# Sliding-window attention and a feed-forward layer on one core: the fourth chunk's scores as fp16 pairs, planned durations and two weight steps changed

## The chip, the core and the metric

The kernel runs on one core of a Trainium2 chip. The metric is device time in microseconds (us) of one execution; lower is better. Three runs of the kernel before gave 631.44, 631.64 and 631.9 us, median 631.64 us. About 0.2% (1.3 us) is what a measurement of this kernel can tell from no change.

## The reference

```python
# q, k, v: (4, 8, 768, 64) float32, n_sink = 4, window = 128
scores = q @ k.T / sqrt(64)
keep = (key < n_sink) | (0 <= query - key < window)
a = softmax(where(keep, scores, -1e9))
x = (a @ v) transposed to (3072, 512)
h = x @ w_in                      # (512, 2048)
g = where(h > 0, h, exp(min(h, 0)) - 1)
out = g @ w_out                   # (2048, 512)
```

The two weights come as 64-bit floats; q, k and v as 32-bit floats.

## The kernel before, in words

**Tiles and chunks.** The 3072 tokens are 24 tiles of 128, cut into nine chunks (`SIZES`, line 43): three of two tiles, then six of three. For each chunk, `attention(c)` (line 495) makes the rows of x, 4 pairs of heads one after the other, and `feed_forward(c, f0, f1, start)` (line 753) runs over 16 blocks of 128 hidden units: `stage1` (line 759) makes h in 12 products of x with a block of w_in, the ELU follows on ACT, DVE and POOL (lines 773 to 786), and `stage2` (line 788) adds the block's products with w_out into one PSUM bank per tile. Both layers work on fp16 pairs: a 32-bit value is kept as a high fp16 half and the fp16 rest, and three products stand for one. Chunks 0 and 1 are cut in two parts (`PARTS`, line 46), so that their first blocks can run while later weights are still being prepared. Attention of a chunk runs beside the feed-forward of the chunk before it.

**Scores.** `DUP` (line 50) says how a chunk's scores are made. In the first `DUP` chunks (line 513 and lines 598 to 601), keys and queries of two heads are loaded as 32-bit floats, one head in partitions 0 to 63, the other in 64 to 127, and used as they are: two fp32 products for a tile and a pair of heads, both listed under line 601. In the later chunks each head has a load of its own (line 523) with the head in both halves of the partitions; ACT writes the high halves (line 524), DVE the rests of the keys (line 525) and of the queries (line 526), and each head's scores are two fp16 products (lines 595 and 596). With `DUP` = 4 the fourth chunk (three tiles, 12 pairs of tile and head pair) is the last with fp32 scores. At the end of the program `check_kq` (line 842) loads the keys and queries of the later chunks again and takes their largest value (line 851).

**Softmax.** DVE adds the mask and takes the extremum (line 616), ACT the exponential with its sum (line 618), a small step scales the sum (line 622, on ACT or POOL) and DVE inverts it (line 623). In chunk 0 POOL builds a diagonal matrix of the inverses (line 630), PE turns the weights with it (line 636), and ACT or DVE evacuates (line 640). In the later chunks ACT and DVE write fp16 pairs (lines 668, 669), POOL the sink columns (lines 675 to 679), and a DMA transposes (line 687). PE multiplies with the values (lines 653 and 701 to 706), and ACT and DVE write x as a pair (lines 739, 740).

**Weights.** `weights(k)` (line 441) prepares 32 pieces of 128 x 512. A 512 KB load on SP's queue (line 314) is followed by four steps: ACT turns the top bits into a fp16 number (line 307, in `weight_f32`), DVE ors the other bits into it, which gives a 32-bit float (line 308), ACT writes the high half (line 456), and POOL the rest in two halves of 256 columns (line 457).

**The order.** Nothing of this order is written by hand. Each step is a task with an engine, an assumed duration and its dependencies (`add`, line 112); `or_=` names a second engine that may take it. `Plan.order` (line 138) works backward for due times and forward for start times, PE's tasks in fixed lines by position, the others by due time, in 8 rounds, and keeps the plan that ends first. What it found is then the fixed order of every engine and of SP's queue: an engine runs its instructions in this order, and one that waits holds all behind it. In a plan, POOL and those steps of DVE that are marked `slow` over 1 take turns (lines 249 to 267). Where the plan sees PE idle for over 0.8 us in its first 100 us, `with_idle_products` (line 896) fills 0.6 of the gap with products of a constant that nobody reads (line 882).

**The end.** One branch at the end (line 1142) skips a general path that takes over when inputs are out of range. `HINTS` (line 891) says how many tasks before the end of each engine's program an instruction is placed that tells the engine of that branch ("notice" below; `keep_order`, line 930). The profile lists it as BRANCH_PREFETCH_HINT on line 1168.

Of the kernel before, what the change touches and what calls it, by code (L numbers as in the profile page):

```python
# [10 lines left out]
F16 = mybir.dt.float16  # L11
# [9 lines left out]
P = 128  # L21
# [27 lines left out]
VISIT = 3  # L49
DUP = 4  # L50
AHEAD = 5
# [4 lines left out]
T_AT = 3.5  # L56
PE_T, PE_V = 0.25, 0.25
RINGS = dict(tp=2, tp_=2, kqs=2, kq=3, vs=2, vm=2, vt=6, sk=2, e=3, st=6, pq=3, pt=6, g=2, gh=3, x=7, wv=4, s=2, po=1, h=2, wu=2, sv=2, wps=1, raw=6)
# [225 lines left out]
def act_us(n, scaled=False):  # L284
    return 0.17 + 0.00088 * n + (0.08 if scaled else 0.0)
# [80 lines left out]
def fast_path(tc, ctx, first, kq, vx, wt, out, low, spread, numbers, flag):  # L366
# [74 lines left out]
    def weights(k):  # L441
        raw, v = raws[slot("raw")], wv[slot("wv")]

        top = wu[k % RINGS["wu"]]
        ld = add("SP", 0.4, lambda: load_weights(nc, raw, wt[k]), deps=[w_done.get(k - AHEAD, [None])[0]], lat=1.45)
        if wide:
            steps = weight_f32(nc, v, top, raw, 2.0)
            a = add("ACT", act_us(512), steps[0], deps=[ld])
            b = add("DVE", 0.13 + 0.00108 * 512, steps[1], deps=[a], slow=1.5)
            ring("wu", [a], [b])  # L450
            ring("raw", [ld], [a, b])
        else:
            a = b = add("ACT", act_us(512), lambda: nc.scalar.activation(v, raw[:, :512].bitcast(F32), AF.Copy, scale=W_SCALE), deps=[ld])
            ring("raw", [ld], [a])

        th = add("ACT", act_us(512), lambda: nc.scalar.activation(w[k][:, 0, :], v, AF.Copy), deps=[b])  # L456
        tls = [add("POOL", pool_us(256), lambda c=c: nc.gpsimd.tensor_tensor(w[k][:, 1, c], v[:, c], w[k][:, 0, c], ALU.subtract), deps=[th]) for c in (slice(0, 256), slice(256, 512))]  # L457
        tl = tls[-1]
        ring("wv", [b], tls)
        w_done[k] = th, *tls  # L460
# [34 lines left out]
    def attention(c):  # L495
# [74 lines left out]
        for p in range(NP):  # L570
# [5 lines left out]
            for g in ts:  # L576
# [47 lines left out]
                if c < PLAIN:  # L624
# [12 lines left out]

                    dgs = add("POOL", pool_us(2 * P), diagonal, deps=[rr])
                    tr = add("PE", PE_T * 2 * nb, turned, deps=[dgs], pos=at[k] + T_AT, line=3)
# [32 lines left out]
                if t >= 2:  # L672

                    def sinks(e3=e3, rs=rs, tmp=tmp, pq=pq):
                        nc.gpsimd.tensor_tensor(tmp, e3[:, :, 0:NS], rs.unsqueeze(2).to_broadcast([P, 2, NS]), ALU.mult)
                        hi = pq[:, 8, 0:96].rearrange("p (g r) -> p g r", g=3)[:, :, 0 : 2 * NS]
                        flat = tmp.rearrange("p e k -> p (e k)")
                        nc.gpsimd.tensor_copy(hi[:, 0:3:2, :], flat.unsqueeze(1).to_broadcast([P, 2, 2 * NS]))
                        nc.gpsimd.tensor_tensor(hi[:, 1, :], flat, hi[:, 0, :], ALU.subtract)

                    b = add("POOL", 0.65, sinks, deps=[rr], lock=False)
                    parts.append(b)
                    his.append(b)
# [54 lines left out]
            to_x = X_SCALE / P_SCALE if c < PLAIN else PO_SCALE  # L738
            fa = add("ACT", act_us(qc, True), lambda xh=xh, po=po, to_x=to_x: nc.scalar.activation(xh, po[:, :qc], AF.Copy, scale=to_x), deps=[vals[-1]])
            fb = add("DVE", dve_us(qc) + 0.1, lambda xh=xh, xl=xl, po=po, to_x=to_x: nc.vector.scalar_tensor_tensor(xl, po[:, :qc], to_x, xh, ALU.mult, ALU.subtract), deps=[fa])  # L740
            ring("po", [vals[0]], [fa, fb])
# [148 lines left out]

HINTS = dict(PE=8, ACT=120, DVE=120, SP=25)
E = mybir.EngineType
# [279 lines left out]
```

## Time and profile before

| what | value |
| --- | --- |
| time, median of 3 runs | 631.64 us |
| profiled execution, its own time | 632.12 us |
| its span in the trace | 630.3 us |
| PE busy, share of the span | 608.5 us, 97% |
| DVE, ACT, POOL busy | 451.4, 418.8, 291.2 us |
| chain that ended last: PE's share | 90% |
| products of the constant (line 882) | 29 |

A span is from the first to the last instruction of the trace; 1.8 us of the profiled execution lie around it. Engines: PE does matrix products, DVE, ACT and POOL work element by element, SP issues the DMAs. A PE that is busy can be waiting inside a product, so the distance from one product's start to the next is the better measure of what it costs.

### The profile page before, as it was taken

The page shows a single profiled execution, that of the slowest core. Times are in us where ns is not written, and L with a number is a line of the kernel's source. Part 1 is how long each engine was busy: PE and PEld are TensorE (multiplying, and loading weights), DVE is VectorE, ACT ScalarE, POOL GpSimd, SP SyncE. Part 2 cuts the span into 40 slices and gives each one's busy share as a digit, 9 for nine tenths or more (in the row PEclk, how much of TensorE's full clock was granted, in tenths as well). Part 3 has the DMA queues.
Part 4 walks back from the last instruction along what each step waited for, and adds up shares of the span by engine and source line. Part 5 has one row for each costly group of instructions (what it writes and reads, how often), then busy time and mean ns, then how long its engine had stood idle before and what let it go on. Part 6 is the DMA issues. An engine that isn't in the chain of part 4 may idle for free.

```text
span 630.3 us, 13327 instructions
## 1 busy us (share of the span) xinstructions
PE 608.5 (97%) x4504; PEld 357.1 (57%) x4504; DVE 451.4 (72%) x1187; ACT 418.8 (66%) x1192; POOL 291.2 (46%) x586
## 2 busy tenths in 40 slices
PE   6897999999999999999999999999999999999995
PEld 4564665666666555555555555555555555555552
DVE  7876677868678766688788889788778887542223
ACT  5888887978678866677667767676776676332221
POOL 4885699864345444344334444334334444222221
PEclk9998999999999999999999999999999999999998
DMA  8697967656546765486458865676556854511001
GB/s 288 212 254 189 305 233 208 161 165 176 120 120 137 194 104 103 88 220 174 103 168 189 208 158 148 145 193 144 154 118 134 220 130 100 124 56 30 0 2 54
DMA packets 120863, 95.06 MB, mean 151 GB/s; under 512 B 98132, under 2 KB 98132, under 8 KB 120788
## 3 DMA queue, kind: packets, MB, share of 16 engines
q1 hardware_dynamic: 120788, 94.14, 58.5%
q8 instruction: 37, 0.61, 0.4%
q14 instruction: 38, 0.31, 0.2%
HBM read 63.18 MB, written 7.34 MB: 112 GB/s over the span
## 4 chain that ended last, share of the span: by engine, by line
PE 90%; POOL 4%; DVE 2%; issue 2%; DMA 1%; ACT 0%; POOLq 0%; DVEq 0%; ACTq 0%
PE acc L793 39%; PE h L765 38%; PE po L701 5%; PE s L601 3%; PE s L595 2%; PE s L596 2%; POOL w L457 2%; DMA pt<-pq 1%; PE h L882 1%; DMA vs<-in_vx_dram 1%; POOL pq L630 1%; PE po L706 1%; DVE pt L334 0%; PE acc L636 0%; DVE wv L308 0%
## 5 line engine op out<-in xcount | busy, mean ns | idle before, releaser
L765 PE MATMUL h<-x,w 128*128 128x384 f16 (+1 forms) x1728 | 275.0, 309 | 1.5 <-DVE g L776 1.5
L765 PEld LDWEIGHTS <-w 128*128 128x128 f16 x1728 | 167.8, 98 | 94.9 <-issue 3.4
L786 POOL TENSOR_TENSOR gl<-g,gh 128x384 f16<-128x384 f32 (+1 forms) x144 | 126.0, 876 | 164.1 <-ACT gh L779 142.4
L793 PE MATMUL acc<-w,gh 128*128 128x512 f16 x768 | 192.8, 379 | 1.0 <-POOL w L457 1.0
L773 ACT ACTIVATE g<-h 128x384 f32<-128x384 f32 (+1 forms) x144 | 65.2, 453 | 102.2 <-PE h L765 93.0
L793 PEld LDWEIGHTS <-gh 128*128 128x128 f16 x768 | 72.4, 98 | 70.8 <-ACT g L773 1.4
L793 PE MATMUL acc<-w,gl 128*128 128x512 f16 x384 | 109.2, 379 | 0.0
L669 DVE SCALAR_TENSOR_TENSOR pq<-e,st,pq 128x256 f16<-128x256 f32 (+1 forms) x176 | 95.5, 569 | 15.0 <-ACT pq L668 14.7
L618 ACT ACTIVATE e<-e,st 128x264 f32<-128x264 f32 (+1 forms) x192 | 92.9, 485 | 14.9 <-DVE st L616 14.0
L779 ACT ACTIVATE gh<-g 128x384 f16<-128x384 f32 (+1 forms) x144 | 69.5, 482 | 45.2 <-DVE g L776 43.3
L616 DVE CUSTOM_DVE_ANT_0 e<-s,m 128x264 f32<-128x264 f32 (+1 forms) x192 | 71.8, 405 | 32.8 <-PE s L596 21.5
L776 DVE SCALAR_TENSOR_TENSOR g<-g,h 128x384 f32<-128x384 f32 (+1 forms) x144 | 72.9, 506 | 14.2 <-POOL g L775 12.4
L668 ACT ACTIVATE pq<-e,st 128x256 f16<-128x256 f32 (+1 forms) x176 | 77.5, 482 | 5.1 <-DVE st L623 4.3
L775 POOL TENSOR_SCALAR g<-g 128x384 f32<-128x384 f32 (+1 forms) x79 | 43.2, 547 | 79.1 <-ACT g L773 75.8
L775 DVE TENSOR_SCALAR g<-g 128x384 f32<-128x384 f32 (+1 forms) x65 | 27.1, 417 | 69.0 <-ACT g L773 68.9
L793 PEld LDWEIGHTS <-gl 128*128 128x128 f16 x384 | 37.5, 98 | 46.7 <-POOL gl L786 0.9
L457 POOL TENSOR_TENSOR w<-wv,w 128x256 f16<-128x256 f32 x64 | 48.9, 786 | 6.1 <-ACT w L456 5.5
L524 ACT ACTIVATE kq<-kqs 128x912 f16<-128x912 f32 (+1 forms) x40 | 35.8, 912 | 15.9 <-PE s L596 13.6
L622 POOL TENSOR_SCALAR st<-st 128x2 f32<-128x2 f32 x76 | 19.1, 251 | 49.4 <-ACT e L618 46.0
L701 PE MATMUL po<-pt,vh 128*64 128x128 f16 x656 | 36.1, 222 | 3.4 <-DVE x L740 1.9
L618 ACT ACTIVATION_READ_ACCUMULATOR e<-e,st 128x1 f32 x192 | 36.1, 188 | 0.0
L701 PEld LDWEIGHTS <-vh 128*64 128x64 f16 x656 | 26.6, 109 | 14.6 <-issue 14.0
(92 smaller groups left out, 619.4 us busy)
## 6 DMA issues: line engine op xcount, KB each, us to landing
raw<-in_wt_dram SPq DMA_DIRECT2D x32, 512.0 KB, 4.6
kqs<-in_kq_dram SPq DMA_DIRECT2D x24, 456.0 KB, 3.9
kqs<-in_kq_dram SPq DMA_DIRECT2D x20, 390.0 KB, 3.6
vs<-in_vx_dram SPq DMA_DIRECT2D x28, 256.0 KB, 3.8
out_dram<-wv SPq DMA_DIRECT2D x24, 256.0 KB, 3.0
vm<-in_kq_dram SPq DMA_DIRECT2D x24, 228.0 KB, 4.2
vm<-in_vx_dram SPq DMA_DIRECT2D x6, 768.0 KB, 5.3
vm<-in_kq_dram SPq DMA_DIRECT2D x16, 195.0 KB, 3.7
```

Of the source, the lines that this page charges most:

```text
L616: red = add("DVE", 0.24 + 0.001 * wd, lambda ee=ee, me=me, sp=sps[e], m=m, wd=wd, to_score=to_score: nc.vector.tensor_tensor_reduce(ee, sp ...
L618: ex = add("ACT", 0.47 + 0.00085 * wd, lambda ee=ee, me=me, rs=rs[:, e : e + 1]: nc.scalar.activation(ee, ee, AF.Exp, bias=me, scale=-1.0, ...
L668: a = add("ACT", act_us(nb * P, True), lambda src=src, hi=hi, re=re: nc.scalar.activation(hi, src, AF.Copy, scale=re), deps=[rr])
L669: b = add("DVE", 0.478 if nb == 2 else 0.33, lambda src=src, hi=hi, lo=lo, re=re: nc.vector.scalar_tensor_tensor(lo, src, re, hi, ALU.mult ...
L701: nc.tensor.matmul(po[e * D : (e + 1) * D, oc], vts[i][x][:, vo : vo + D], pt[:, (2 * e + part) * nb + i, :], start=new, stop=last)
L765: nc.tensor.matmul(hp[:, :n], win[:, part, d, :], xx[:, :n], start=k == 0, stop=k == 3 * ND - 1)
L773: a = add("ACT", act_us(n) + 0.18, lambda gf=gf, hp=hp, sums=sums: nc.scalar.activation(gf, hp[:, :n], AF.Exp, scale=1.0 / G_SCALE, accum_ ...
L775: b = add("DVE", 0.14 + 0.00057 * n, lambda gf=gf: nc.vector.tensor_scalar(gf, gf, -1.0, G_SCALE, ALU.add, ALU.mult), deps=[a], slow=2.1, ...
L776: b = add("DVE", dve_us(n), lambda gf=gf, hp=hp: nc.vector.scalar_tensor_tensor(gf, gf, 0.0, hp[:, :n], ALU.min, ALU.max), deps=[b])
L779: th = add("ACT", act_us(n), lambda gf=gf, gh=gh: nc.scalar.activation(gh[:, :n], gf, AF.Copy), deps=[b])
L786: tls.append(add("POOL", pool_us(cut), lambda gl=gl, gf=gf, gh=gh, cut=cut: nc.gpsimd.tensor_tensor(gl[:, :cut], gf[:, :cut], gh[:, :cut], ...
L793: nc.tensor.matmul(acc[i], gg[:, i * P : (i + 1) * P], wout[:, part, :], start=f == f0 and k == 0, stop=f == f1 - 1 and k == 2)
```

## The change

- `DUP` goes from 4 to 3: the fourth chunk's scores become fp16 pairs. Its keys and queries come in 8 loads instead of 4, each followed by lines 524, 525 and 526, and `check_kq` has 4 more pairs of loads and 4 more maxima.
- Line 307's step may run on POOL too (after the change listed under line 448), and line 456's on DVE. In the order that results, POOL has 12 of the 32 top steps and DVE 7 of the 32 high halves.
- Assumed durations are changed: the value products of chunk 0 (`PE_V`), lines 307, 308 and 457, the diagonal, the sinks, lines 739 and 740. The steps of the instructions themselves stay as they were.
- The notices move: ACT's 108 tasks before its end instead of 120, SP's 50 instead of 25.
- With the durations, the whole order changes; the products of line 882 go from 29 to 70.

```diff
-DUP = 4
+DUP = 3
...
-PE_T, PE_V = 0.25, 0.25
+PE_T, PE_V = 0.25, 0.13
...
         if wide:
             steps = weight_f32(nc, v, top, raw, 2.0)
-            a = add("ACT", act_us(512), steps[0], deps=[ld])
-            b = add("DVE", 0.13 + 0.00108 * 512, steps[1], deps=[a], slow=1.5)
+            a = add("ACT", 0.77, steps[0], deps=[ld], or_=("POOL", 0.85, lambda: nc.gpsimd.tensor_scalar(top.bitcast(F16)[:, 1::2], raw.bitcast(BF16)[:, 4:2049:4], 2.0, None, ALU.mult)))
+            b = add("DVE", 0.8, steps[1], deps=[a], slow=1.5)
...
-        th = add("ACT", act_us(512), lambda: nc.scalar.activation(w[k][:, 0, :], v, AF.Copy), deps=[b])
-        tls = [add("POOL", pool_us(256), lambda c=c: nc.gpsimd.tensor_tensor(w[k][:, 1, c], v[:, c], w[k][:, 0, c], ALU.subtract), deps=[th]) for c in (slice(0, 256), slice(256, 512))]
+        th = add("ACT", act_us(512), lambda: nc.scalar.activation(w[k][:, 0, :], v, AF.Copy), deps=[b], slow=1.5, or_=("DVE", 0.55, lambda: nc.vector.tensor_copy(w[k][:, 0, :], v)))
+        tls = [add("POOL", 0.75, lambda c=c: nc.gpsimd.tensor_tensor(w[k][:, 1, c], v[:, c], w[k][:, 0, c], ALU.subtract), deps=[th]) for c in (slice(0, 256), slice(256, 512))]
...
-                    dgs = add("POOL", pool_us(2 * P), diagonal, deps=[rr])
+                    dgs = add("POOL", 0.8, diagonal, deps=[rr])
...
-                    b = add("POOL", 0.65, sinks, deps=[rr], lock=False)
+                    b = add("POOL", 0.9, sinks, deps=[rr], lock=False)
...
-            fa = add("ACT", act_us(qc, True), lambda xh=xh, po=po, to_x=to_x: nc.scalar.activation(xh, po[:, :qc], AF.Copy, scale=to_x), deps=[vals[-1]])
-            fb = add("DVE", dve_us(qc) + 0.1, lambda xh=xh, xl=xl, po=po, to_x=to_x: nc.vector.scalar_tensor_tensor(xl, po[:, :qc], to_x, xh, ALU.mult, ALU.subtract), deps=[fa])
+            fa = add("ACT", act_us(qc) - 0.03, lambda xh=xh, po=po, to_x=to_x: nc.scalar.activation(xh, po[:, :qc], AF.Copy, scale=to_x), deps=[vals[-1]])
+            fb = add("DVE", dve_us(qc), lambda xh=xh, xl=xl, po=po, to_x=to_x: nc.vector.scalar_tensor_tensor(xl, po[:, :qc], to_x, xh, ALU.mult, ALU.subtract), deps=[fa])
...
-HINTS = dict(PE=8, ACT=120, DVE=120, SP=25)
+HINTS = dict(PE=8, ACT=108, DVE=120, SP=50)
```

How instructions move, at three places. On PE, one tile and head pair of the fourth chunk (the buffers `kqs` hold keys and queries as loaded, `kq` their fp16 pairs, `s` the scores), before:

```order
L765 MATMUL h_168<-x,w_148 128x256
L601 MATMUL s_170<-kqs_63 128x264
L601 MATMUL s_171<-kqs_63 128x264
L793 LDWEIGHTS gh_115
L793 MATMUL acc_173<-w_145,gh_115 128x512
```

and now, for a tile and head pair of the same chunk:

```order
L793 MATMUL acc_174<-w_139,gl_118 128x512
L595 LDWEIGHTS kq_78
L595 MATMUL s_170<-kq_78 128x264
L596 LDWEIGHTS kq_78
L596 MATMUL s_170<-kq_78 128x264
L595 LDWEIGHTS kq_76
L595 MATMUL s_171<-kq_76 128x264
L596 LDWEIGHTS kq_76
L596 MATMUL s_171<-kq_76 128x264
L765 LDWEIGHTS w_144
```

Two fp32 products of the raw load became four fp16 products of the split buffers; both kinds stand between products of the feed-forward. On POOL, the first steps after the setup (`pq<-ident,st` is chunk 0's diagonal, `w<-wv,w` the rest of a weight, `wu<-raw` the top step), before:

```order
L622 TENSOR_SCALAR st_98<-st_98 128x2
L630 TENSOR_TENSOR pq_104<-ident,st_98 128x256
L622 TENSOR_SCALAR st_99<-st_99 128x2
L630 TENSOR_TENSOR pq_105<-ident,st_99 128x256
L622 TENSOR_SCALAR st_100<-st_100 128x2
L457 TENSOR_TENSOR w_136<-wv_124,w_136 128x256 x2
L630 TENSOR_TENSOR pq_106<-ident,st_100 128x256
```

and now:

```order
L622 TENSOR_SCALAR st_98<-st_98 128x2
L448 TENSOR_SCALAR wu_128<-raw_130 128x512
L630 TENSOR_TENSOR pq_104<-ident,st_98 128x256
L630 TENSOR_TENSOR pq_105<-ident,st_99 128x256
L448 TENSOR_SCALAR wu_129<-raw_131 128x512
L448 TENSOR_SCALAR wu_128<-raw_132 128x512
L630 TENSOR_TENSOR pq_106<-ident,st_100 128x256
L457 TENSOR_TENSOR w_136<-wv_124,w_136 128x256
```

The first three top steps now stand on POOL between chunk 0's diagonals, and the sums of the second and third step of the softmax (line 622) went to ACT. On SP's queue, around the notice, before (row 242; the branch is row 271):

```order
L523 DMA kqs_63<-in_kq_dram 128x912
L819 DMA out_dram<-wv_127 128x512
L687 DMA_TRANSPOSE pt_109<-pq_106 128x9x128
L819 DMA out_dram<-wv_124 128x512
L1168 BRANCH_PREFETCH_HINT
L819 DMA out_dram<-wv_125 128x512
```

and now (row 225; the branch is row 279):

```order
L523 DMA kqs_63<-in_kq_dram 128x912
L848 DMA vm_93<-in_kq_dram 64x912 x2
L687 DMA_TRANSPOSE pt_107<-pq_104 128x4x128
L1168 BRANCH_PREFETCH_HINT
L687 DMA_TRANSPOSE pt_108<-pq_105 128x8x128
L523 DMA kqs_64<-in_kq_dram 128x912
```

SP's notice moved 17 rows toward the start, from 29 rows ahead of its branch to 54.

## Rows read from the trace of the kernel before

**Rows 1.** Windows: stretch, width, busy (count) per engine, PE's clock share, DMA.

```profile
core 0: us, PE busy (x) PEld busy (x) DVE busy (x) ACT busy (x) POOL busy (x), PEclk, DMA share, GB/s
4.50:66.00 61.50, 52.51 (x429) 34.03 (x429) 47.90 (x164) 48.87 (x142) 42.13 (x85) 0.97 0.86 249
66.00:200.00 134.00, 132.65 (x1078) 85.47 (x1077) 98.52 (x264) 107.98 (x324) 83.67 (x158) 1.00 0.65 179
130.00:190.00 60.00, 60.00 (x505) 38.27 (x503) 43.66 (x134) 45.36 (x151) 25.74 (x56) 1.00 0.58 143
...
90.00:100.00 10.00, 10.00 (x69) 6.22 (x67) 9.03 (x20) 8.72 (x24) 9.47 (x18) 1.00 0.61 175
```

**Rows 2.** PE's waits over the span: engine, line waited for, us, times, longest.

```profile
PE acc L636 <- POOL pq L630: 2.1, 2, 1.3
PE po L701 <- DVE x L740: 1.9, 1, 1.9
PE h L765 <- DVE g L776: 1.5, 2, 1.1
...
PE acc L793 <- POOL w L457: 1.0, 2, 0.6
```

**Rows 3.** Timeline of PE: start us, duration us, line and product.

```profile
141.94 0.59 PE L793 MATMUL acc<-w,gl 128*128 128x512 f16 x2
142.46 0.71 PE L601 MATMUL s<-kqs 64*128 64x264 f32 x4
143.11 1.48 PE L765 MATMUL h<-x,w 128*128 128x256 f16 x12
...
145.29 0.59 PE L793 MATMUL acc<-w,gl 128*128 128x512 f16 x2
...
146.25 1.48 PE L765 MATMUL h<-x,w 128*128 128x256 f16 x12
...
191.35 0.59 PE L793 MATMUL acc<-w,gl 128*128 128x512 f16 x2
191.78 0.28 PE L595 MATMUL s<-kq 128*128 128x264 f16 x1
...
192.24 1.47 PE L765 MATMUL h<-x,w 128*128 128x256 f16 x12
```

**Rows 4.** Groups by line and shape: busy us, mean ns of one, idle before.

```profile
L457 POOL TENSOR_TENSOR w<-wv,w 128x256 f16<-128x256 f32 x64 | 48.9, 786 | 6.1 <-ACT w L456 5.5
L775 POOL TENSOR_SCALAR g<-g 128x384 f32<-128x384 f32 x57 | 32.6, 572 | 66.0 <-ACT g L773 66.0
L307 ACT ACTIVATE wu<-raw 128x512 f16<-128x512 bf16 x32 | 24.1, 771 | 2.7 <-DMA raw<-in_wt_dram 2.7
L526 DVE SCALAR_TENSOR_TENSOR kq<-kqs,kq 64x384 f16<-64x384 f32 x40 | 23.9, 599 | 0.6
L775 DVE TENSOR_SCALAR g<-g 128x384 f32<-128x384 f32 x39 | 14.2, 363 | 60.4 <-ACT g L773 60.4
L524 ACT ACTIVATE kq<-kqs 128x780 f16<-128x780 f32 x16 | 13.4, 846 | 6.4 <-PE s L596 4.1 <-PE s L595 2.3
L775 DVE TENSOR_SCALAR g<-g 128x256 f32<-128x256 f32 x26 | 13.0, 498 | 8.6 <-ACT g L773 8.5
L525 DVE SCALAR_TENSOR_TENSOR kq<-kqs,kq 128x396 f16<-128x396 f32 x16 | 9.3, 583 | 0.3
L882 PE MATMUL h<-hot 128*128 128x240 bf16 x29 | 5.4, 343 | 0.0
```

**Rows 5.** Line 1142's instructions: count, ns min/median/max, first and last start us.

```profile
L1142 SPq EVENT_SEMAPHORE  x8: 17/17/17, 628.4 to 628.9; - x8
...
L1142 DVEq COMPARE_BRANCH  x1: 84/84/84, 624.2 to 624.2; - x1
L1142 DVEq EVENT_SEMAPHORE  x1: 21/21/21, 624.8 to 624.8; - x1
L1142 SPq COMPARE_BRANCH  x1: 78/78/78, 625.4 to 625.4; - x1
```

**Rows 6.** DMA traffic of 627 to 628 us, in 40 slices of 0.025 us.

```profile
GB/s 0 0 82 0 0 0 0 0 82 0 0 82 0 0 82 0 0 0 82 0 0 82 0 0 0 0 0 0 0 0 0 0 0 0 0 0 0 0 0 0
```

## The prediction

> **What bounds the kernel now.** I read the windows first. From 66 to 200 us PE is busy for 132.65 of 134 us, and from 130 to 190 us for all of 60.00 at clock 1.00 [rows 1]: there, and in the rest of the program alike, the time is the sum of PE's products, and work taken from PE is time won. From 4.5 to 66 us it is another kernel: PE works 52.51 of 61.5 us and stands idle for 9.0, while no engine is full (DVE 47.90, which is 78%, ACT 48.87 or 79%, POOL 42.13 or 69%, DMA 0.86) [rows 1]. That stage is bound by the chain from a weight's load over ACT, DVE and POOL to PE, and by the order in which these engines take their steps. The waits of PE say where it hurts: 2.1 us for POOL's diagonals, 1.9 and 1.5 for DVE, 1.0 for a weight's rest on POOL, together 6.5 [rows 2]. The third place is the end: DVE starts its branch at 624.2 us and goes on at 624.8, 0.6 later, but SP branches at 625.4 and has its next event at 628.4, 3.0 later [rows 5].
>
> The sum is made against the profiled execution, 632.12 us; it lies 0.48 above the median of the runs, 631.64, and the forecast is put down by as much.
>
> **Part 1, the scores: -3.4.** Twelve pairs of tile and heads change on PE, 8 with 264 columns and 4 with 132. What one costs is read from distances of starts, since a waiting product counts as busy. After the two L793 products the next product follows in 191.78 - 191.35 = 0.43 us. So two fp32 products of 264 columns take 143.11 - 141.94 - 0.43 = 0.74 us, and two of 132 take 146.25 - 145.29 - 0.43 = 0.53; the four fp16 products of a 264 pair take 192.24 - 191.78 = 0.46 [rows 3]. For 132 columns I take half, 0.23. Saved: 8 x (0.74 - 0.46) + 4 x (0.53 - 0.23) = 2.2 + 1.2 = 3.4 us, where PE has no idle time.
>
> The price lies on other engines. ACT gets 8 steps of line 524 at 0.846, 6.8 us; DVE 8 of line 525 at 0.583 and 8 of line 526 at 0.599, 9.5 us [rows 4]. From 130 to 190 us ACT would go from 45.4 to 52.2 of 60 (87%), DVE from 43.7 to 53.2 (89%) [rows 1]. I cost both at nothing: in 90 to 100 us DVE works 9.03 of 10 us, ACT 8.72 and POOL 9.47 while PE loses nothing [rows 1]. If that cover is gone, the 9.5 us of DVE come onto PE's path (a rival below). The 4 more loads on SP's queue and the 4 more checks near the end have a DMA share of 0.58 to move in [rows 1] and no consumer on PE: nothing.
>
> **Part 2, the weights and the new order up to 66 us: -1.0.** While the first chunks run, 7 top steps of line 307 leave ACT, at 0.771 each: -5.4 us [rows 4]. They come to POOL as line 448, which the trace does not show. The nearest rows are POOL's multiplication of 384 columns, 0.572, and the two halves of line 457, 2 x 0.786 = 1.57, which read two inputs [rows 4]; I take the first, which is the same operation, scaled to 512 columns: 0.76, and 0.8 with a strided output, so POOL gets 7 x 0.8 = +5.6. The small sums that go from POOL to ACT, and the few evacuations and high halves that move between ACT and DVE, I count at nothing, being the smallest steps or as many each way. What remains for PE is bounded below by those four waits all gone, -6.5 [rows 2], and above by POOL's added work fully on the path, +5.6. I take -1.0, a little to the gain's side of the middle, because ACT, relieved by about what POOL gets, is the fuller of the two: 12.6 us free on ACT against 19.4 on POOL [rows 1].
>
> The 41 more constant products take 5.4 / 29 = 0.19 us each [rows 4], 7.6 in all. I cost them at nothing: they have the 9.0 us of idle [rows 1] to lie in. Where a foreseen gap does not occur they push PE; half of them would be 3.8, less than the bound above.
>
> **Part 3, the notices: -0.8.** SP's notice comes 54 rows ahead instead of 29. DVE, whose notice stands far ahead, loses 0.6 us at its branch where SP loses 3.0 [rows 5], so the length of the lead is the likely difference. But what SP then waits for is the last stores, and their last packet moves in slice 21 of 627 to 628 us, at 627.55 [rows 6]. SP's events at 628.4 to 628.9 cannot come before that: the gain is 0.8 to 1.3, or nothing if the notice still comes too late. I take 0.8.
>
> **Sum:** 632.12 - 3.4 - 1.0 - 0.8 = 626.9 in a profiled execution, and **626.4** in the runs.
>
> **Rivals.**
> *The notice still does nothing.* For it: nothing in the trace shows how long a lead SP's queue needs; between 29 rows that failed and 54 there is less than a factor of two. Against it: DVE's 0.6 [rows 5]. Time: 626.4 + 0.8 = 627.2. The Trainium skill, "Runtime: NRT & Kernel Launch", section "Instruction fetch mechanics", says that prefetch is purely sequential and that a taken branch to a target outside the present window forces a fetch before the engine goes on; by that rule no notice helps, and this rival is the outcome. DVE's row, 0.6 against 3.0, disagrees with its strict reading.
>
> *The early waits go away.* The durations that the plan works with are now nearer to the trace (line 457 at 0.75 against 0.786 measured, the top step at 0.77 against 0.771 [rows 4]), so that the order may fit what happens: -6.5 instead of -1.0 [rows 2], 620.9. Against it: chunk 0's diagonals on POOL, the longest of these waits, now share their engine with three of the top steps.
>
> *POOL becomes the early bound.* For it: PE waits for POOL in two of the four rows already [rows 2], and diagonal, top step and rest now alternate on it. +5.6 instead of -1.0 gives 626.4 + 6.6 = 633.0, at the upper edge of no change from 631.64; the small sums that leave POOL, counted at nothing above, bring it inside.
>
> *Slower: the fourth chunk's splits come late.* One mechanism: DVE runs in a fixed order, the 16 new steps stand between the ELUs of the block that PE needs next, and a step held there holds g behind it; PE has 0 us to spare in 130 to 190 us. It decides once DVE's free 16.3 us [rows 1] do not take the 9.5 us (with the high halves that it may also take) at the moments when PE needs them, and costs these 9.5: 626.4 + 9.5 = 635.9. For it: DVE's times stretch beside POOL; its 256-column ELU step takes 0.498 us, longer than the 384-column one with 0.363 [rows 4], the narrow ones being those of the early stage where POOL is fullest. Against it: 90 to 100 us [rows 1]. The Trainium skill, "SBUF — State Buffer", section "Who interferes with whom", says that DVE and GpSimd share a pair of ports as an exclusive lock, and that a DVE instruction with two inputs in SBUF blocks against a GpSimd one that reads SBUF. By that rule lines 525 and 526, and the top steps now on POOL, stretch each other, which speaks for this rival; the 498 against 363 ns agree.
>
> **How the numbers follow.** A measurement of this kernel tells about 0.2%, 1.3 us, from no change. Forecast 0.50; notice without effect 0.17; early waits gone 0.10; these three are faster, 0.77. POOL as the bound 0.11: same. Late splits 0.12: slower. The likeliest case's own range is 624.0 to 629.0. The range reaches down to an early gain of 4.9 us in place of 1.0, 622.5, which leaves out about half of the second rival, and up to 633.0, POOL's full added work, which leaves out the last: some 0.17 outside.
>
> **What would show it.** Right: L601 ends with the third chunk, L595 pairs of the fourth stand 0.46 us apart, and PE's busy time before 66 us apart, falls by 3 us; SP's branch and next event are 0.6 to 2.2 us apart. PE's idle time before 66 us tells part 2: under 9.0 less 1 is a gain, over 14 makes POOL the bound, and then PE waits for lines 448, 457 or 630. Late splits show as PE waits for lines 524 to 526 or 775 between 130 and 200 us, with DVE over 90%. Wrong altogether: a total above 633, or PE's busy share from 66 us on below 97%.

## The result, and the profile after

The changed kernel takes 637.6 us (median of 4 runs, 635.97 to 637.78) where the kernel before took 631.54 beside it: a ratio of 1.0092, interval 1.0078 to 1.0107. It is slower by 6 us; 626.4 had been forecast.

The windows of the changed kernel, the same stretches as [rows 1] and one more, 66 to 130 us (columns as there):

```profile
core 0: us, PE busy (x) PEld busy (x) DVE busy (x) ACT busy (x) POOL busy (x), PEclk, DMA share, GB/s
4.50:66.00 61.50, 52.13 (x411) 34.46 (x411) 43.70 (x146) 41.36 (x130) 49.18 (x78) 0.94 0.81 234
66.00:130.00 64.00, 59.52 (x484) 38.23 (x485) 53.01 (x116) 51.35 (x148) 59.75 (x87) 1.00 0.81 229
130.00:190.00 60.00, 59.69 (x499) 41.08 (x497) 48.81 (x144) 46.40 (x150) 33.37 (x64) 1.00 0.66 155
```

The second of these stretches in the kernel before:

```profile
66.00:130.00 64.00, 62.95 (x488) 40.87 (x487) 46.91 (x104) 54.91 (x152) 53.06 (x91) 1.00 0.72 217
```

POOL is the engine to look at. In the first stretch its busy time goes from 42.13 to 49.18 us, while DVE and ACT go down by 4.2 and 7.5. In the second it works 59.75 of 64 us, 93%, against 53.06 before, and PE, which the forecast had at nearly full rate from 66 us on, stands idle for 4.5 us there, against 1.05 before. In the first stretch PE's busy time hardly moves, 52.13 against 52.51 us, but 65 products of the constant are in it where there were 29; without their busy time, 9.67 against 5.41 us, PE does 4.6 us less of the program's own work there. From 130 to 190 us nothing is lost but 0.3: the new splits of the fourth chunk (DVE 43.66 to 48.81) hold nobody up.

PE's waits of the changed kernel, longest first, but for one of 4.5 us at the start that both kernels have (engine, line waited for, us, times, longest):

```profile
PE acc L793 <- POOL gl L786: 3.1, 2, 1.7
PE h L765 <- POOL w L457: 2.5, 1, 2.5
PE acc L636 <- POOL pq L630: 2.4, 3, 1.3
PE po L653 <- ACT pt L640: 2.2, 1, 2.2
PE s L601 <- DVE st L616: 1.3, 1, 1.3
```

Three of these five name POOL, 8.0 us together against 3.1 in [rows 2]. And the group of the new step, with the other weight steps (line, engine, shapes, count; busy us, mean ns of one; idle before):

```profile
L457 POOL TENSOR_TENSOR w<-wv,w 128x256 f16<-128x256 f32 x64 | 51.8, 828 | 0.7 <-ACT w L456 0.2
...
L448 POOL TENSOR_SCALAR wu<-raw 128x512 f16<-128x512 bf16 x12 | 20.3, 1704 | 1.4 <-DMA raw<-in_wt_dram 1.1
...
L307 ACT ACTIVATE wu<-raw 128x512 f16<-128x512 bf16 x20 | 15.4, 775 | 3.3 <-DMA raw<-in_wt_dram 3.3
...
L456 DVE CAST w<-wv 128x512 f16<-128x512 f32 x7 | 3.7, 525 | 0.0
```

POOL's top step takes 1.70 us: twice the 0.85 that the plan assumes, twice the 0.8 of the forecast, 2.2 times what ACT needs for the same. Twelve of them are 20.3 us of POOL. The chain that ended last shows where they stand (start us, us, what):

```profile
9.05 1.69 POOL wu L448
10.74 0.84 POOL pq L630 x2
11.58 0.70 issue
12.29 3.29 POOL wu L448 x2
15.60 1.06 DVE wv L308
```

Two of chunk 0's diagonals (line 630), which PE's first turnings need, stand behind one top step, and the next two top steps stand before the third; 5.0 of these 6.5 us of POOL go to top steps.

**The scores** (timeline of PE: start us, duration us): two of their places in the fourth chunk, to be held against [rows 3]. Each line is one product; the other three of a pair are left out.

```profile
141.11 0.22 PE L595 MATMUL s<-kq 128*128 128x132 f16 x1
...
141.34 1.47 PE L765 MATMUL h<-x,w 128*128 128x256 f16 x12
...
145.25 0.28 PE L595 MATMUL s<-kq 128*128 128x264 f16 x1
...
145.70 0.59 PE L793 MATMUL acc<-w,gh 128*128 128x512 f16 x2
```

A pair with 132 columns takes 0.23 us and one with 264 takes 0.45; 0.23 and 0.46 had been forecast.

**The end** (line 1142, as in [rows 5]):

```profile
L1142 SPq EVENT_SEMAPHORE  x8: 17/17/17, 632.0 to 634.4; - x8
...
L1142 SPq COMPARE_BRANCH  x1: 78/78/78, 631.4 to 631.4; - x1
```

SP goes on 0.6 us after its branch, not 3.0, and from its branch to the end of the span it takes 635.8 - 631.4 = 4.4 us where it took 4.9.

**The clock** has a second dip. In two-microsecond windows (columns as above), PE's granted clock between 8 and 70 us is below 0.99 in these of the changed kernel:

```profile
26.00:28.00 2.00, 1.88 (x9) 0.88 (x10) 0.60 (x1) 1.45 (x7) 1.84 (x2) 0.52 0.06 23
28.00:30.00 2.00, 2.00 (x13) 1.80 (x13) 1.98 (x7) 1.10 (x4) 1.55 (x3) 0.63 0.41 96
...
50.00:52.00 2.00, 1.88 (x10) 1.33 (x10) 1.94 (x7) 1.42 (x5) 1.14 (x3) 0.50 1.04 181
52.00:54.00 2.00, 2.00 (x20) 1.11 (x20) 1.39 (x5) 1.06 (x4) 1.37 (x4) 0.66 0.68 217
```

The kernel before has one such dip, at 52 to 56 us. At 0.50 the clock is at 1.2 GHz, the lower of its two levels. Ahead of each of the two dips of the changed kernel PE had stood nearly still: it works for 0.00 of the 2 us from 24 to 26, and for 0.11 us from 49 to 50. Each dip is some 3.4 us at half speed, which loses up to 1.7 us of work.

### The profile page after: what moved, and what is told of

It reads as the page before. It is cut to its first block, busy times and chain, and to the rows that moved or that the text cites. A ratio compares the mean times of both kernels' runs of the same rounds, so it can differ in the third digit from the quotient of the medians.

```text
span 635.8 us, 13444 instructions
## 1 busy us (share of the span) xinstructions
PE 610.4 (96%) x4545; PEld 362.0 (57%) x4545; DVE 467.3 (73%) x1207; ACT 414.4 (65%) x1185; POOL 320.9 (50%) x601
## 4 chain that ended last, share of the span: by engine, by line
PE 86%; POOL 6%; DMA 5%; issue 1%; DVE 1%; ACT 0%; SPq 0%; POOLq 0%; ACTq 0%
PE acc L793 37%; PE h L765 37%; PE po L701 5%; PE s L595 2%; PE s L596 2%; DMA pt<-pq 2%; POOL wu L448 2%; DMA raw<-in_wt_dram 2%; POOL w L457 1%; PE s L601 1%; POOL gl L786 1%; PE po L706 1%; DVE wv L308 0%; POOL st L675 0%; DMA kqs<-in_kq_dram 0%
## 5 line engine op out<-in xcount | busy, mean ns | idle before, releaser
L786 POOL TENSOR_TENSOR gl<-g,gh 128x384 f16<-128x384 f32 (+1 forms) x144 | 127.4, 886 | 155.0 <-ACT gh L779 132.6
L775 POOL TENSOR_SCALAR g<-g 128x384 f32<-128x384 f32 (+1 forms) x83 | 45.7, 551 | 67.9 <-ACT g L773 67.2
L524 ACT ACTIVATE kq<-kqs 128x780 f16<-128x780 f32 (+1 forms) x48 | 43.0, 903 | 16.3 <-PE s L596 13.3
L457 POOL TENSOR_TENSOR w<-wv,w 128x256 f16<-128x256 f32 x64 | 51.8, 828 | 0.7 <-ACT w L456 0.2
L622 POOL TENSOR_SCALAR st<-st 128x2 f32<-128x2 f32 x75 | 20.5, 273 | 51.8 <-ACT e L618 48.9
L595 PE MATMUL s<-kq 128*128 128x264 f16 (+1 forms) x144 | 34.4, 267 | 0.6 <-DVE st L616 0.6
```

Source lines behind the costliest of these rows:

```text
L775: b = add("DVE", 0.14 + 0.00057 * n, lambda gf=gf: nc.vector.tensor_scalar(gf, gf, -1.0, G_SCALE, ALU.add, ALU.mult), deps=[a], slow=2.1, ...
L786: tls.append(add("POOL", pool_us(cut), lambda gl=gl, gf=gf, gh=gh, cut=cut: nc.gpsimd.tensor_tensor(gl[:, :cut], gf[:, :cut], gh[:, :cut], ...
```

## The experiments

Three theories stood against each other. **A**: POOL's top step, at twice its price, makes POOL the bound of the first 130 us. **B**: the new order as such (new durations, more constant products) costs the time, whoever takes the steps. **C**: the splits of the fourth chunk hold PE. Every time below is a median beside runs of the kernel before on the same chip (631.2 to 631.8), with its ratio and interval. One thing holds for all of them: an edit of a price, of an engine's alternative or of `DUP` makes the plan anew, so that the whole order can change with it. Only the notices, the number of constant products and the form of an instruction can be changed with the order kept.

### Each part by itself

The top steps back on ACT, every other setting as changed:

```diff
-            a = add("ACT", 0.77, steps[0], deps=[ld], or_=("POOL", 0.85, ...))
+            a = add("ACT", 0.77, steps[0], deps=[ld])
```

> The changed kernel with line 307's step on ACT alone (no second engine for it), all else as changed; the plan then gives DVE 14 of the high halves and has 88 constant products. Theory A (POOL's top step takes 1.69 us in the changed kernel's trace, 12 of them 20.3 us, and makes POOL the bound up to 130 us): the loss of about 9.5 us there goes, 637.6 - 9.5 = 628, within 626 to 630. Theory B (the new durations and the order with 70 or more constant products cost the time, whoever takes the top steps): 636 to 639. Theory C (the fourth chunk's splits hold PE): also unchanged, 636 to 639.

**627.19 us**, 0.9952 (0.9935 to 0.9969). In this kernel PE's waits for POOL shrink to 0.3 us, and it works through from 66 us on:

```profile
4.50:66.00 61.50, 56.00 (x478) 37.76 (x480) 51.92 (x172) 51.52 (x155) 45.27 (x86) 1.00 0.94 269
66.00:130.00 64.00, 64.00 (x515) 42.32 (x510) 52.40 (x118) 52.04 (x145) 54.84 (x84) 1.00 0.76 218
```

Without this one alternative the whole loss is gone, as A has it; B and C had 636 to 639. But the plan found another order without it (DVE has 14 of the high halves, and there are 88 products), so this run does not part POOL's work from the order that came with it.

The kernel before with fp16 scores in the fourth chunk alone:

```diff
-DUP = 4
+DUP = 3
```

> The kernel before with the fourth chunk's scores as fp16 pairs and nothing else; 29 constant products as before. Theory A, and the prediction's part 1: 631.5 - 3.4 = 628.1, within 627.5 to 629. Theory C: the splits cost what they save or more, 631 or above. Theory B says nothing of it beyond 628.1.

**628.24 us**, 0.9958 (0.9944 to 0.9972), 3.3 us faster: part 1 of the prediction by itself. PE's busy time up to 130 us is that of the kernel before (52.56 and 62.95 us in the two stretches), so the gain lies behind it. C falls.

The kernel before with POOL allowed for line 307's step and nothing else:

```diff
-            a = add("ACT", act_us(512), steps[0], deps=[ld])
+            a = add("ACT", act_us(512), steps[0], deps=[ld], or_=("POOL", 0.85, ...))
```

> The kernel before with POOL allowed for line 307's step at the assumed 0.85 us and nothing else; the plan then gives POOL 19 of the 32. Theory A: 19 x 1.69 = 32 us of POOL's time where it has some 30 free up to 130 us: slower than before by 6 to 15 us, 638 to 647. Theory B: the old durations are kept, so near before, 630 to 633.

**646.22 us**, 1.0246 (1.0233 to 1.0260). Nineteen steps of 1.71 us, 32.5 us of POOL (and 50 products):

```profile
66.00:130.00 64.00, 60.23 (x466) 37.41 (x463) 47.91 (x100) 47.54 (x133) 61.02 (x90) 0.96 0.82 219
```

POOL is busy for 95% of this stretch, and here too PE has idle time in it. The alternative does its harm with the old durations too: A again, and B, which had 630 to 633 here, falls in so far as it blames the new durations. The order is a new one here as well.

The kernel before with the notices alone:

```diff
-HINTS = dict(PE=8, ACT=120, DVE=120, SP=25)
+HINTS = dict(PE=8, ACT=108, DVE=120, SP=50)
```

> The kernel before with the notices moved as in the change and nothing else. Prediction's part 3: SP goes on 0.6 us after its branch instead of 3.0, and the end comes 0.8 us earlier, 630.7. From the changed kernel's trace, where the time from DVE's branch to the end of the span is 5.5 us against 6.1, all three theories expect -0.6, 630.9. If the notice does nothing: 631.5.

**631.09 us**, 0.9988 (0.9976 to 1.0000): 0.4 us, at the edge of what can be told. Its profile is clearer: SP's branch at 626.6 is followed by its first event at 627.1, and from the branch to the end of the span it takes 4.1 us in place of 4.9, the 0.8 of part 3. In the profiles of all kernels here with the moved notices SP goes on 0.5 to 0.6 us after its branch, and in the three without them 3.0 to 3.1. The Trainium skill ("Runtime: NRT & Kernel Launch", section "Instruction fetch mechanics") has prefetch purely sequential; by that the notice could do nothing, and SP's 0.5 against 3.0 us disagrees.

The change with neither second engine:

```diff
-            a = add("ACT", 0.77, steps[0], deps=[ld], or_=("POOL", 0.85, ...))
+            a = add("ACT", 0.77, steps[0], deps=[ld])
...
-        th = add("ACT", act_us(512), ..., deps=[b], slow=1.5, or_=("DVE", 0.55, ...))
+        th = add("ACT", act_us(512), ..., deps=[b])
```

> The changed kernel with neither second engine: top steps and high halves all on ACT, so what is left of the change is the fourth chunk's fp16 scores, the new durations and the notices; 45 constant products. Without the notices and the durations the fp16 scores alone gave 628.2, and the notices about 0.5. If the durations are worth nothing: 627.7. If they are what makes 627.2 of the kernel with the high halves still shared: 627.2 or below. If the high halves on DVE are worth something: 628 to 630.

**628.96 us**, 0.9959 (0.9945 to 0.9974). Its interval overlaps those of the two kernels at 627.2 and 628.2: what the high halves on DVE and the new durations are worth without POOL's steps is not shown.

### The wrong price, or the work?

```diff
-or_=("POOL", 0.85,
+or_=("POOL", 1.7,
```

> The changed kernel with one number different: the plan assumes 1.7 us instead of 0.85 for POOL's top step. It still gives POOL 11 of the 32 (12 in the change). Theory A1 (the harm is the wrong price: the plan put the steps where it thought POOL had room): with the right price about as good as with the steps on ACT, 627.2, within 626 to 630. Theory A2 (the harm is the work itself, 11 x 1.69 = 18.6 us more on POOL, wherever the plan puts it): 633 to 638.

**628.76 us**, 0.9962 (0.9948 to 0.9977). The plan still gives POOL 11 steps, and each still takes 1.76 us on the mean; POOL is as full as in the change (60.34 of 64 us from 66 to 130), but PE loses 1.3 us there and not 4.5. By the expectation this is A1: 8.8 of the 10.4 us are gone with the work still there. So the harm was mostly the order's. Whether the wrong price made that order poor is another question, since a kernel with another price is a kernel with another order; it is taken up under "What is the rest?".

### Why 1.69 us?

A price list: 18 instructions on POOL whose results nobody reads, ahead of the program (the first is the changed kernel's step; the next has only the input strided, then only the output, then neither; the last two are 32-bit products of 512 and 256 columns):

```diff
+    for _ in range(3):
+        nc.gpsimd.tensor_scalar(d16[:, 1::2], s16[:, 4:2049:4], 2.0, None, ALU.mult)
+        nc.gpsimd.tensor_scalar(d16[:, 0:512], s16[:, 4:2049:4], 2.0, None, ALU.mult)
+        nc.gpsimd.tensor_scalar(d16[:, 1::2], s16[:, 0:512], 2.0, None, ALU.mult)
+        nc.gpsimd.tensor_scalar(d16[:, 0:512], s16[:, 0:512], 2.0, None, ALU.mult)
+        nc.gpsimd.tensor_scalar(dst.bitcast(F32), src.bitcast(F32)[:, 0:512], 2.0, None, ALU.mult)
+        nc.gpsimd.tensor_scalar(dst.bitcast(F32)[:, 0:256], src.bitcast(F32)[:, 0:256], 2.0, None, ALU.mult)
```

> A price list: the kernel with the top steps on ACT, and 18 more POOL instructions at the start whose results nobody reads, three each of six forms: the top step as changed (16-bit input at every fourth place, 16-bit output at every second, 512 columns), the same with only the input strided, with only the output strided, with neither, and a 32-bit multiplication of 512 and of 256 columns. Its own time means nothing. If strides make the 1.69 us: the form with neither takes 0.7 to 0.8 us and one of the strided ones 1.69. If 16-bit numbers make it: all four take 1.69 and the 32-bit one about 0.75. If it is the length alone: the 32-bit one with 512 columns takes 1.69 as well.

The rows of the lines 420 to 424, in the order of the diff (count, then ns shortest/median/longest, first and last start):

```profile
L420 POOL TENSOR_SCALAR dst<-src x3: 1647/1661/1678, 4.7 to 43.1; 128x512 f16<-128x512 bf16 x3
L421 POOL TENSOR_SCALAR dst<-src x3: 1513/1517/1965, 10.4 to 45.9; 128x512 f16<-128x512 bf16 x3
L422 POOL TENSOR_SCALAR dst<-src x3: 1623/1632/1804, 12.8 to 47.6; 128x512 f16<-128x512 bf16 x3
L423 POOL TENSOR_SCALAR dst<-src x3: 1487/1487/1487, 14.7 to 49.3; 128x512 f16<-128x512 bf16 x3
L424 POOL TENSOR_SCALAR dst<-src x3: 1922/1927/1929, 17.8 to 51.7; 128x512 f32<-128x512 f32 x3
```

Neither the strides nor the 16-bit numbers are the cause: without strides it still takes 1.49, and with 32-bit numbers 1.93. Yet POOL's step on line 775 takes 0.57 for 384 columns [rows 4]. One thing that differs is that line 775 does two operations in one instruction, a sum and a product. The second list, in the same place:

```diff
+        nc.gpsimd.tensor_scalar(d16[:, 1::2], s16[:, 4:2049:4], 2.0, 1.0, ALU.mult, ALU.mult)
+        nc.gpsimd.tensor_scalar(d16[:, 1::2], s16[:, 4:2049:4], 0.0, 2.0, ALU.add, ALU.mult)
+        nc.gpsimd.tensor_scalar(d32[:, 0:384], s32[:, 0:384], 2.0, None, ALU.mult)
+        nc.gpsimd.tensor_scalar(d32[:, 0:384], s32[:, 0:384], 2.0, 1.0, ALU.mult, ALU.mult)
+        nc.gpsimd.tensor_scalar(d32[:, 0:384], s32[:, 0:384], -1.0, 2.0, ALU.add, ALU.mult)
+        nc.gpsimd.tensor_scalar(d32[:, 0:384], s32[:, 0:384], 2.0, None, ALU.add)
```

> A second price list, again 18 more POOL instructions at the start whose results nobody reads, three each of six forms: the top step as times 2 times 1, the top step as plus 0 times 2, and 32-bit steps of 384 columns as one product, as two products, as a sum and a product (the form of line 775, which takes 0.57 us), and as one sum. Its own time means nothing. If one operation is what is slow: the forms with two take 0.55 to 0.85 us, the single ones 1.2 to 1.5. If a sum is what is fast: the two forms that begin with a sum and the single sum are short, the products long. If line 775 is fast only because it writes where it reads, all six are long.

The rows of its lines 421 to 426, in the order of the diff:

```profile
L421 POOL TENSOR_SCALAR dst<-src x3: 757/777/1213, 4.7 to 29.6; 128x512 f16<-128x512 bf16 x3
L422 POOL TENSOR_SCALAR dst<-src x3: 752/815/941, 5.6 to 32.4; 128x512 f16<-128x512 bf16 x3
L423 POOL TENSOR_SCALAR dst<-src x3: 1174/1175/1183, 10.7 to 35.8; 128x384 f32<-128x384 f32 x3
L424 POOL TENSOR_SCALAR dst<-src x3: 508/948/1014, 12.0 to 38.5; 128x384 f32<-128x384 f32 x3
L425 POOL TENSOR_SCALAR dst<-src x3: 508/509/512, 13.1 to 39.6; 128x384 f32<-128x384 f32 x3
L426 POOL TENSOR_SCALAR dst<-src x3: 1169/1170/1180, 14.6 to 40.3; 128x384 f32<-128x384 f32 x3
```

With one operation, product or sum, 384 columns take 1.17 us; with two they take 0.51: the instruction that does less is 2.3 times as slow. The top step goes from 1.66 to 0.78 (times 2, times 1) or 0.82 (plus 0, times 2). Two of line 424's three were stretched to 0.95 and 1.01: these two, at 12.0 and 38.5 us, run beside steps of DVE with two tensor inputs (lines 563 and 308 of that kernel), and the third, of 0.51, beside none.

The changed kernel with the second of these forms, same values, same order:

```diff
-raw.bitcast(BF16)[:, 4:2049:4], 2.0, None, ALU.mult)
+raw.bitcast(BF16)[:, 4:2049:4], 0.0, 2.0, ALU.add, ALU.mult)
```

> The changed kernel with POOL's top step written as plus 0 times 2 instead of times 2; the same values, the same order, 12 of them on POOL. If the step then takes 0.7 to 0.85 us, as the plan assumes: the loss before 130 us goes and the time is 626 to 628, the forecast's 626.4 by its own steps. If it still takes 1.69: 637.6.

**632.85 us**, 1.0024 (1.0010 to 1.0037). The steps take 0.80 on the mean, a little less than the plan's 0.85, and 4.75 us come back; but the 626 to 628 of the expectation is missed by 5. This run changes the step alone and keeps the change's order: the price explains 4.75 of the 10.4 us.

### What is the rest?

The 12 runs of that kernel go from 629.8 us at a mean clock of 0.999 to 635.5 at 0.988, so PE's clock was one suspect. What holds it is shown by taking all constant products out of the kernel with the top steps on ACT:

```diff
-IDLE_US, IDLE_FILL, IDLE_UNTIL, IDLE_LEAST = 0.11, 0.6, 100.0, 0.8
+IDLE_US, IDLE_FILL, IDLE_UNTIL, IDLE_LEAST = 0.11, 0.6, 100.0, 1000.0
```

> The kernel with the top steps on ACT (627.2 us, 88 constant products) with no products of the constant at all, the order otherwise the same. Prediction: they lie in idle time and cost nothing; then 627. If they sit on PE's path: up to 88 x 0.14 = 12.7 us earlier at most, 622 to 626. If what they give is PE's clock (granted 1.00 from 4.5 to 66 us with 88, 0.94 to 0.97 in the profiles with 29 and 70): later, 629 to 634, with the clock of that stretch below 0.97.

**631.04 us** (627.1 to 635.6 in 12 runs, clock 0.984 to 0.992) instead of 627.19. Before 30 us PE is busy for 21.43 of 25.5 us instead of 24.60, and then, from 26 to 34 us, its clock stands at about half for some 7 us, among them:

```profile
28.00:30.00 2.00, 2.00 (x10) 1.73 (x10) 1.14 (x2) 1.19 (x4) 1.92 (x4) 0.50 0.94 318
30.00:32.00 2.00, 2.00 (x13) 1.04 (x10) 1.52 (x6) 0.73 (x3) 0.74 (x2) 0.50 0.88 350
```

The products are worth 3.9 us here; the prediction had its 41 more at nothing. How much of the 3.9 is the clock is not told apart: three of PE's waits grow as well (for the transposing DMA from 2.7 to 4.0 us, for line 616 from 0.5 to 2.9, for line 630 from 0.3 to 1.7). Then more of them should help the kernel at 632.85 (gaps from 0.5 us filled to nine tenths: 129 products), and the one at 627.19 (141):

```diff
-IDLE_US, IDLE_FILL, IDLE_UNTIL, IDLE_LEAST = 0.11, 0.6, 100.0, 0.8
+IDLE_US, IDLE_FILL, IDLE_UNTIL, IDLE_LEAST = 0.11, 0.9, 100.0, 0.5
```

> The changed kernel with POOL's top step in two operations and 129 instead of 70 products of the constant (gaps from 0.5 us on are filled to nine tenths, instead of from 0.8 us to six tenths); the order of all else stays. If the rest of the loss (632.85 against 627.2) is PE's clock: near its fastest run with 70, 629.8, within 628.5 to 630.5, with less scatter and a clock of 0.997 or more. If it is the waits for POOL: 632 to 633. If the products are now too many and push PE: above 633.

> The kernel with the top steps on ACT and 141 instead of 88 products, filled in the same way. Its runs with 88 went from 626.5 at a clock of 0.997 to 629.7 at 0.993 to 0.996. If the clock makes the scatter: a median of 626.0 to 627.0 with less scatter. If 141 products push PE: 628 to 632.

**632.1 us**, 1.0014 (1.0003 to 1.0025), and **631.25**, 1.0003 (0.9991 to 1.0015). The first holds the clock (0.994 to 0.999) and wins nothing; the second loses 4 us. A product takes 0.117 us (12 in 1.41 us in one place of the timeline), so 53 more are 6.2 us: in such numbers they most likely push PE, and what the clock gives the first kernel may have gone there. These two do not settle the clock's share.

Two more kernels with the step in two operations ask for the order's share: one has the order made for steps of 1.7 us, the other the plan's price at the measured 0.78.

```diff
-or_=("POOL", 0.85, ... 2.0, None, ALU.mult)
+or_=("POOL", 1.7, ... 0.0, 2.0, ALU.add, ALU.mult)
```

```diff
-or_=("POOL", 0.85, ... 2.0, None, ALU.mult)
+or_=("POOL", 0.78, ... 0.0, 2.0, ALU.add, ALU.mult)
```

> The order made for a top step of 1.7 us on POOL (11 of 32, 82 products, 628.8 us with steps that take 1.69), with the step in two operations that take 0.78: 10 us less on POOL before 130 us and nothing else changed. If POOL's work on these steps still costs time in that order: 626 to 628, the best of all. If the order hid them wholly: 628.8 as it was.

> The changed kernel with the step in two operations and the plan's price for it at the measured 0.78 instead of 0.85 (12 on POOL, 10 high halves on DVE, 50 products). If the rest of the loss in e15 (632.85) were a question of this price: 627 to 629. If the plan is as blind to the waits at 0.78 as at 0.85, which is the more likely for so small a step: 630 to 634.

**625.96 us**, 0.9918 (0.9905 to 0.9930), 0.8% below the kernel before; and **626.27**, 0.9907 (0.9890 to 0.9923), not to be told from it, which its expectation had held unlikely. With a price that differs by 0.07 us the planner finds an order that is 6.6 us better (12 steps on POOL still, 10 high halves on DVE and not 7, 50 products). The longest of PE's waits in that kernel name POOL no more; 0.2 us for line 630 are left of it:

```profile
PE s L601 <- DVE st L616: 2.9, 2, 2.2
PE po L701 <- DVE x L740: 1.6, 2, 0.9
PE po L701 <- DMA pt<-pq: 1.3, 2, 1.0
PE po L653 <- ACT pt L640: 0.3, 1, 0.3
```

The kernel at 632.85 still had 4.1 us of such waits (1.6 for line 457, 1.3 for 786, 1.2 for 630), though its profile is of the shortest of its 12 runs, 629.8. And a full POOL is not enough to hold PE: with the price of 0.78 POOL is fuller from 66 to 130 us than in the change, 61.60 us or 96%, and PE loses 0.3 us there:

```profile
66.00:130.00 64.00, 63.69 (x494) 41.63 (x493) 57.31 (x120) 54.27 (x155) 61.60 (x89) 1.00 0.83 247
```

The clock does not explain the difference: at clocks of 0.993 to 0.995 the runs with 0.85 lie at 631.65 to 634.06 and those with 0.78 at 625.75 to 627.91. The rest is thus the order that the plan happened to find at 0.85. The times side by side, in us, by the order (rows) and by what a top step on POOL takes (columns):

| order made for a step of | one operation, 1.70 to 1.76 us | two operations, 0.80 to 0.85 us |
| --- | --- | --- |
| 0.85 | 637.6 (the change) | 632.85 |
| 1.7 | 628.76 | 625.96 |
| 0.78 | not run | 626.27 |

Along a row the slow step costs 4.75 or 2.8 us; down a column the order costs 6.6 to 8.8. The order made for 0.85 is the poor one even where the steps take about what it assumes, and the order made for 1.7 is as good as any where they take half of that. So a wrong price is not what makes an order poor here. Theory B was thus right in part: this order costs time with quick steps too. Why the planner found a worse one at 0.85 stays open; its search was not looked into.

### Two that led nowhere

One more chunk's scores as fp16 pairs, on the kernel at 627.19:

```diff
-DUP = 3
+DUP = 2
...
-        check_kq(..., exps_done[NF * 6 - 4 + 2 * i])
+        check_kq(..., exps_done[NF * 6 - 12 + 2 * i])
```

> The kernel with the top steps on ACT (627.2 us) with the third chunk's scores as fp16 pairs too (the checks of the keys begin 4 blocks earlier so that they have room). Two tiles, 8 pairs of tile and heads, some 0.28 us each where PE is the bound: 627.2 - 2.2 = 625.0. If the splits of the keys (16 steps on DVE, 8 on ACT, some 15 us together) fall in the stage before 130 us where DVE and POOL are near full: nothing won, 627 to 630.

**630.74 us**, 0.9983 (0.9969 to 0.9997), 3.5 us worse. The splits fall in the early stage: PE now waits 1.1 us for line 526 and 0.9 for line 668, and 3.9 us for the transposing DMA. What was free for the fourth chunk is not for the third.

The kernel before with the fourth chunk's fp16 scores, the notices and 69 products:

```diff
-DUP = 4
+DUP = 3
...
-IDLE_US, IDLE_FILL, IDLE_UNTIL, IDLE_LEAST = 0.11, 0.6, 100.0, 0.8
+IDLE_US, IDLE_FILL, IDLE_UNTIL, IDLE_LEAST = 0.11, 1.0, 100.0, 0.4
...
-HINTS = dict(PE=8, ACT=120, DVE=120, SP=25)
+HINTS = dict(PE=8, ACT=108, DVE=120, SP=50)
```

> The kernel before, its old durations and order, with the fourth chunk's scores as fp16 pairs (628.2 alone), the moved notices (0.4 to 0.8) and 69 instead of 29 products (gaps from 0.4 us on filled whole). If the products hold the clock here too: 626 to 627.5, as good as the new order. If the clock was no loss in this order: 627.5 to 628. If they push PE: 629 or above.

**629.32 us**, 0.9970 (0.9958 to 0.9982), not to be told from the fourth chunk's scores alone. More products gave that order nothing; 629 or above was to mean that they push PE.

## Why the prediction was wrong

**Part 1, the scores, -3.4: right.** Alone 3.3 us, and the pairs measure 0.45 and 0.23. The rival of late splits, which would have given nearly the measured time (635.9), is not what happened: no wait of PE in the changed kernel names lines 524 to 526. The rule of the Trainium skill that was set beside it ("SBUF — State Buffer", section "Who interferes with whom") is borne out where the two engines meet. Two of line 526's steps in the changed kernel, with POOL's steps around them:

```profile
138.20 1.77 POOL L457 TENSOR_TENSOR w<-wv,w 128x256 f16<-128x256 f32 x2
139.45 0.93 DVE L526 SCALAR_TENSOR_TENSOR kq<-kqs,kq 64x384 f16<-64x384 f32 x1
139.93 0.98 POOL L786 TENSOR_TENSOR gl<-g,gh 128x256 f16<-128x256 f32 x1
...
152.88 0.56 DVE L526 SCALAR_TENSOR_TENSOR kq<-kqs,kq 64x384 f16<-64x384 f32 x1
```

Of its first six steps after 130 us, the three beside POOL's lines 457 and 786 take 0.91 to 0.93 us and the other three 0.56 to 0.58. They meet too seldom for it to cost much: the mean over the program goes from 599 to 626 ns, 1.3 us in 48 steps. The row that the prediction set beside the rule, 498 against 363 ns, is of line 775, which has one tensor input, and so it does not bear on a rule for two.

**Part 3, the notices, -0.8: right in kind.** From branch to end the time shrinks by 0.8 us in the kernel with the notices alone and by 0.5 in the change; in medians 0.4, at the edge of what can be told.

**Part 2, the weights and the new order, -1.0: wrong, and two of its steps failed.**

The first is the price of line 448. "I take the first, which is the same operation, scaled to 512 columns: 0.76, and 0.8 with a strided output": line 775 is not the same operation. It does two in one instruction, and the top step does one, which costs 1.70. Seven steps would thus be 11.9 us and not 5.6, and in the trace nine of the twelve start before 66 us, 15.2 us. In the order as it was planned this price cost 4.75 us. The text had the better row in its hand, two halves of line 457, 1.57; it set it beside the other and let go of it, for the bound above was worked out from 0.8. With 7 x 1.57 = 11.0 in its place the range would have ended at 626.4 + 1.0 + 11.0 = 638.4 and held the result, though with some luck, since the price is less than half of the miss.

The second is the new order. The prediction put its worth between all four waits gone and POOL's added work fully on the path, and so counted work by engine and idle time by stage. But the order found at 0.85 costs 6.6 us against the one found at 0.78 with the same quick steps, and no term and no rival stands for that. 4.75 and 6.6 together are about the miss of 11.2. What in that order is poor stays open.

The rival "POOL becomes the early bound" had the waits right, three of PE for POOL and all. But its price was made from seven steps at 0.8, and its 633.0 lies 4.6 us short. Its sign, over 14 us of idle time of PE before 66 us, did not come either: it was 61.5 - 52.13 = 9.4, because products of the constant count as busy and part of the loss fell behind 66 us.

The 41 more products, costed at nothing, are not free of effect: in the kernel with the top steps on ACT, leaving all 88 out cost 3.9 us, and 53 more cost 4.1. What the 41 did in the change itself is not shown.

The forecast's 626.4 is about what the change comes to with the step in two operations and its price at 0.78, 626.27. That is in another order, and so no proof of the forecast's terms.

## What to carry to other kernels

When an operation moves to an engine on which the trace has no row for it, take the price from the far end of the rows until a row of the very same instruction form exists, and carry both ends through to the range; a probe of a few instructions settles it. In a kernel whose order is planned from assumed durations, the order that the planner finds can cost more than the work that was moved: here 6.6 us against 4.75, and a price that differs by 0.07 us decided it. So a plan made with the right durations can still be a poor one: try a few prices and time each plan. A slack price (1.7 for a step of 0.8) did as well here as the measured one, 625.96 and 626.27. And compare kernels with the order kept before a cause is named: the run with the right price of 1.7 alone looked as if the wrong price had done it all.

## What was not expected of the hardware

A TENSOR_SCALAR instruction on POOL with one arithmetic operation is slower than one with two: 1.17 against 0.51 us for 384 columns of 32-bit floats, 1.66 against 0.78 to 0.82 for the top step. And in the kernel with the top steps on ACT, whose profile shows a clock of 1.00 from 4.5 to 66 us, the clock without the constant products stood at about half for some 7 us of that stretch, and the time rose by 3.9 us and scattered over 8.5.
